# RWKV6 attention into a two-layer block: one more pair of feature tiles by 15 products in the last block, its sums two steps later, its copies on GpSimd

## The chip, the cores and the metric

One core of one Trainium2 chip. The metric is the device time of one execution in microseconds (us), the median of several runs. A profile is one more execution, recorded by the hardware.

## The reference

```
state = wt[:, :, :, None] * state + kt (x) vt          # attention, 768 positions in sequence
y[:, :, t] = rt . (state + (u * kt) (x) vt)
x = y as (3072 tokens, 384)
h = x @ w_in                                            # w_in 384 x 2048
g = h - tanh(h)
out = g @ w_out                                         # w_out 2048 x 384
```

All of it is float32. There are 4 batches, 8 heads, 768 positions and a head size of 48, so x has 3072 rows of 384.

## The kernel before, in words

**Blocks and steps.** The 3072 tokens are cut into eight blocks of 384 tokens (L1112, L1261). A block has 16 steps (L1271), one for each tile of 128 features; step f of a block is written as f 12, f 13 and so on below. In a step TensorE multiplies the block's x with one tile of w_in (`first`, L881 to L888: three matmuls of 128x384, in the PSUM tile hp). ScalarE copies hp to h. From h, ScalarE and VectorE make g (`slight`, L894 to L918). In most steps the squares are ScalarE's (lines 906, 907 and 909). In the last two steps of the last block the square s = h*h is VectorE's, with a maximum beside it (the line 914), and only then ScalarE squares once more (L917). Then come two VectorE products of 128x384 (L891): h = h*s, and g from qa and h. These two are put off by a step: they stand in the list `rest` of the next step.

**The second layer in two forms.** g @ w_out is done plainly (`Second`, L954 to L995): for each of three tiles of 128 tokens a matmul of 128x384 a feature tile, the third split into two of 192. Or it is done for a pair of feature tiles at once (`Fewer`, L997 to L1063): the 3x2 blocks of g and the 2x3 blocks of w_out are added and subtracted beforehand (VectorE, L932 for g, `form_g`), then come 15 products of 128x128 in place of 18 (`product`, L1004). Each of the 15 has a place of its own and is accumulated over all pairs. Products 0 to 11 lie in the PSUM banks acc (`add`, L1013, in two parts of six), 12 to 14 in a bank of att (`others`, L1025). At the end of all pairs ScalarE copies the banks to the tile `sums` (L1023), `others_summed` (L1037) adds the last three, and the 12 VectorE operations of `SUMS` (L113, run at L1046) turn the 15 places into nine blocks of 128x128, which `PLACES` (L119) lists.

**The last block.** Blocks 1 to 6 take `Fewer` for all 16 steps. The last takes it for f 0 to 9, five pairs (`LAST = 5`, L75, L234), and plain for f 10 to 15. So its sums must be joined: once they are ready `gathered` (L1054) copies the nine blocks into rows in the tile G (six copies), and `added` (L982) adds those rows at the last feature tile (L993, VectorE, one input from PSUM, one from G) and sends the rows out (L995).

**What sets the order.** TensorE, VectorE, ScalarE and SyncE run their instructions in the order in which the program writes them (`manual_schedule`, L1114); GpSimd is not in that list, but a data dependence holds for it too. In each step the program writes the step's `first`, then VectorE's list `ops`, then what is `due`. A product of a pair, or a plain feature tile, is due two steps after its g is begun (L1315, L1317). L1299 to L1305 choose how `rest`, the forms and the others are woven in `ops`; `between(a, b)` takes one of each in turn. At L1324 to L1331 the last block gets its `others`, its sums in two halves and its copies. At f 14 come three VectorE operations that test earlier results (L1334, L1250, L1251). After the last step come two more of them (L1384), a matmul of one column that counts (L1386), the last `rest`, and `again` (L1389), which the engines read at L1393 ahead of the second and third tile of tokens. The last two plain feature tiles are written there, tile of tokens by tile of tokens (L1395).

Of the kernel before, what the change touches and what calls it, by code (L numbers as in the profile page):

```python
# [68 lines left out]
NF = FF // P  # L69
# [2 lines left out]
AHEAD = 6  # L72
RAWS = 5
LAG = 2
LAST = 5  # L75
PIECES = 0, 0, 2, 3, 3, 2, 4, 4, 3, 3, 3, 4, 4
UNITS = [(0, 0), (0, 1)] + [u for j in range(NF // 2 - 2) for u in ((1, j), (0, j + 2))] + [(1, NF // 2 - 2),
                                                                                      (1, NF // 2 - 1)]
# [34 lines left out]
SUMS = (("sub", (15, 6, 10), (0, 0, 6)), ("sub", (2, 2, 5), (3, 5, 3)),  # L113
        ("add", (6, 7, 13), (1, 7, 1)), ("add", (7, 9, 14), (5, 9, 11)),
        ("sub", (10, 10, 14), (5, 5, 6)), ("add", (11, 12, 11), (10, 2, 10)),
        ("sub", (14, 4, 14), (11, 3, 11)), ("add", (2, 8, 13), (10, 5, 10)),
        ("add", (13, 4, 13), (2, 2, 15)), ("add", (8, 8, 12), (4, 4, 12)),
        ("add", (0, 4, 0), (11, 2, 11)), ("sub", (14, 14, 1)))
# [8 lines left out]
def kernel(  # L127
# [12 lines left out]
    nc = tc.nc  # L140
# [46 lines left out]
    def draw(names, cols):  # L187
        nc.gpsimd.memset(mask_all[0:L, cols], 1.0)
        for m in names:
# [5 lines left out]
            else:  # L195
# [10 lines left out]
                   in_=start[:, 0:BANK].unsqueeze(1).to_broadcast([P, 2 * NPAIR * NCP * L // BANK, BANK]))  # L206
# [26 lines left out]
    fast = range(1, blocks_n)  # L233
    few = [0 if i not in fast else NF if i + 1 < blocks_n else 2 * LAST for i in range(blocks_n)]  # L234
    n_whole = blocks_n * NPAIR * NCH
# [62 lines left out]
    def scratch(ps):  # L298
        return ps.tile([P, 2, BANK], F32, name="att", tag="att")
# [594 lines left out]
    def slight(h, n, i, f):  # L894

        s, qa = (dense.tile([P, NB], F32, name=name, tag=name) for name in ("s", "qa"))
        q, j = divmod(f, 2)
        if i in fast:  # L900
            g = G[:, g_at(q, "0" + "ab"[j]):g_at(q, "2" + "ab"[j]) + 1].rearrange("p t c -> p (t c)")
        else:
            g = ring(sums, 0, n)
        if n in light:
            at = 2 * blocks_n + light.index(n)
            nc.scalar.activation(out=s, in_=h, func=AF.Square)  # L906
            nc.scalar.activation(out=qa, in_=s, func=AF.Square, bias=shift[:, 4:5])  # L907
            junk = work.tile([P, UP * NCH * LP], BF16, name="junk", tag="junk", bufs=1)
            nc.scalar.activation(out=junk[:, 0:NB], in_=s, func=AF.Relu, bias=shift[:, 5:6],  # L909
                                 accum_out=excess[:, at:at + 1])  # L910
            square = first = []
        else:
            at = plain.index(n)
            square = [lambda: nc.vector.tensor_tensor_reduce(
                out=s, in0=h, in1=h, scale=1.0, scalar=0.0, op0=ALU.mult, op1=ALU.max,
                accum_out=top[:, at:at + 1])]
            first = [lambda: nc.scalar.activation(out=qa, in_=s, func=AF.Square, bias=shift[:, 4:5])]  # L917
        return g, first, square, [product(h, h, TOP, s, ALU.mult), product(g, qa, REST, h, ALU.add)]  # L918
# [78 lines left out]
    class Fewer:  # L997
# [56 lines left out]
        def gathered(self):  # L1054

            for i, k, n, src in self.pieces():
                nc.scalar.copy(out=G[:, 6 + 3 * i + k:6 + 3 * i + k + n], in_=src)
            return [G[:, 6 + 3 * i:9 + 3 * i].rearrange("p t c -> p (t c)") for i in range(NB // P)]

        def store(self):  # L1060
# [67 lines left out]
    def converting(pieces, n):  # L1128

        made = []  # L1130
        for _ in range(n):
            if not pieces:
                on_act, on_dve = convert(*raws.pop(0))
                pieces += zip(on_act, ([], [], on_dve))
            op, then = pieces.pop(0)
            op()
            made += then
        return made
# [95 lines left out]
    ahead_of_h, rest, formed, extra, behind, due, summed = [], [], [], [], [], [], []  # L1234
    held_back, forming, late = [], [], []

    def between(ops, others):

        n = min(len(ops), len(others))
        return [op for pair in zip(ops, others) for op in pair] + ops[n:] + others[n:]  # L1240
# [12 lines left out]
    def form_w(n, q, k):  # L1253

        by = w_out_sb.rearrange("p (q j) (k c) -> p q j k c", j=2, c=P)
        op, *of = W_FORMS[n]
        a, b = (by[:, q:q + k, "ab".index(x[0]), int(x[1])] if isinstance(x, str) else forms[:, q:q + k, x]
                for x in of)
        nc.vector.tensor_tensor(out=forms[:, q:q + k, n], in0=a, in1=b, op=OPS[op])

    for i, blk in enumerate(blocks):  # L1261
# [7 lines left out]
        fewer = Fewer(row0, acc, few[i] // 2) if few[i] else None  # L1269
        second = Second(row0, acc, few[i]) if few[i] < NF else None  # L1270
        for f in range(NF):  # L1271
# [11 lines left out]
            g, ahead_of_h, square, later_ops = slight(h, now, i, f)  # L1283
# [6 lines left out]
                              if of and not name.startswith("bound")]  # L1290
            if i:
                spare += [lambda n=n: form_w(n, 4 if f < 12 else 6, 2) for n in formed_w.get(f, ())]
            if not now:
                ops = square + converting(pieces, 2)
            elif now == 1:
                ops = rest + late + square + converting(pieces, 3)
            elif not i:
                ops = extra + square + (rest + behind + spare if f < 7 else rest[:1] + behind + spare + rest[1:])
            elif forming:  # L1299
                ops = between(rest, forming[:2]) + square + formed + forming[2:]  # L1300
                ops = (between(ops, behind) if len(behind) > 2 else ops + behind) + spare
            elif square:
                ops = (between(rest, behind) if len(behind) > 2 else rest + behind) + square + formed + extra + spare
            else:
                ops = between(rest + formed, behind + spare)  # L1305
            for op in ops:
                op()
            rest, behind, formed, forming, held_back = later_ops, [], [], held_back, []
# [7 lines left out]
            else:  # L1316
                due.append((now + LAG + (not i), second.add if later else second.added, (f, g)))  # L1317
            if fewer and second and f == 2 * LAST:
                sure = scratch(ps_a)
# [3 lines left out]
            if fewer and second:  # L1323
                if f == 2 * LAST + 1:  # L1324
                    fewer.others(ps_a, range(4, LAST))
                    behind.append(fewer.others_summed)
                elif f in (2 * LAST + 2, 2 * LAST + 3):
                    for op in fewer.sum(*((0, 6) if f % 2 == 0 else (6, len(SUMS)))):
                        op()
                elif f == 2 * LAST + 4:  # L1330
                    second.rows = fewer.gathered()  # L1331
            if not later and f == NF - 2:
                at = n_whole + n_excess
# [17 lines left out]
            if i == 0 and f == NF - 3:  # L1351
# [3 lines left out]
                G = wide.tile([P, 32, P], F32, name="g", tag="g")  # L1355
# [31 lines left out]
    for op in ahead_of_h + rest:  # L1387
        op()
    nc.vector.tensor_single_scalar(again, sure[0:1, 0, 0:1], float(P * (n_whole + n_excess + n_top)),  # L1389
                                   op=ALU.not_equal)  # L1390
# [9 lines left out]
    with tc.If(anew > 0, label="anew"):  # L1400
        with tc.manual_schedule(engines={PE, SP, DVE, ACT}), ExitStack() as again_pools:
# [7 lines left out]
            for blk in [Block(b, q) for b in range(B) for q in range(NQ)]:  # L1409
                blk.general(ps_a)  # L1410
                second = Second(blk.b * S + blk.q * NB, acc)
# [56 lines left out]
```

## Time and profile before

| | |
|---|---|
| median of 3 runs | 544.04 us (544.01 to 545.4) |
| the profiled execution | 543.88 us |
| its span in the profile | 542.2 us, so 1.68 us lie around the span |
| TensorE, VectorE, ScalarE, GpSimd busy | 534.0, 459.3, 404.2, 7.0 us |
| granted TensorE clock | 0.999 |

A row of a timeline gives the start, the duration, the engine, the line of the kernel, the operation, what it writes and reads, and the count of instructions put together in the row. In brackets stands the idle time of the engine in front of it and who ended that. An "x6" of TensorE at L883 is three matmuls: each float32 matmul shows two records. PEld is the loading of weights. A line of the chain of waits has start, length, engine, tile, line and records.

### The profile page before, as it was taken

How to read it: one execution, taken by the hardware profiler on the slowest of the kernel's cores; microseconds unless marked ns; L12 is line 12 of the kernel's file. 1: busy time of each engine (PE TensorE's matmuls, PEld its weight loads, DVE VectorE, ACT ScalarE, POOL GpSimd, SP SyncE). 2: the span in 40 equal slices, each digit the busy share in tenths (PEclk: the TensorE clock that was granted, in tenths of full speed). 3: DMA queues.
4: the chain of work that ended last, by engine and by line, in shares of the span. 5: the costliest groups of instructions: out<-in, count | busy, mean ns of one | idle time of the engine just before them, and what ended most of it. 6: DMA issues, size and time to landing. Idle time of an engine off the chain costs nothing.

```text
span 542.2 us, 14874 instructions
## 1 busy us (share of the span) xinstructions
PE 534.0 (98%) x5682; PEld 403.4 (74%) x5682; DVE 459.3 (85%) x943; ACT 404.2 (75%) x814; POOL 7.0 (1%) x51
## 2 busy tenths in 40 slices
PE   8999999999999999999999999999999999999996
PEld 5756665678787777877887787877788788777874
DVE  7999999999989989798997989879797997557563
ACT  4999996897668886688767886688766885766561
POOL 1100000000000000000000000000000000000000
PEclk9999999999999999999999999999999999999999
DMA  7799642342311642154122622135321510100101
GB/s 276 242 403 348 219 119 71 122 112 81 106 48 46 162 118 57 44 148 119 61 56 87 132 92 70 50 102 145 90 84 45 118 31 3 56 1 0 45 1 47
DMA packets 53048, 56.34 MB, mean 104 GB/s; under 512 B 21488, under 2 KB 50928, under 8 KB 52976
## 3 DMA queue, kind: packets, MB, share of 16 engines
q1 hardware_dynamic: 52592, 55.18, 33.5%
q8 instruction: 48, 0.79, 0.6%
q14 instruction: 24, 0.20, 0.1%
q10 hardware_dynamic: 288, 0.10, 0.1%
q0 software_dynamic: 96, 0.07, 0.1%
HBM read 44.73 MB, written 4.72 MB: 91 GB/s over the span
## 4 chain that ended last, share of the span: by engine, by line
PE 95%; DVE 2%; DMA 1%; issue 0%; PEld 0%; SPq 0%; PEldq 0%; DVEq 0%
PE hp L883 44%; PE acc L1011 27%; PE att L1011 7%; PE acc L962 5%; PE att L769 4%; PE att L494 2%; PE acc L989 2%; PE att L575 1%; PE att L883 1%; DMA r<-in_rT 1%; PE acc L883 1%; DVE scores L502 1%; DVE post L429 0%; PE att L989 0%; PEld att L679 0%
## 5 line engine op out<-in xcount | busy, mean ns | idle before, releaser
L883 PE MATMUL hp<-xT,w_sb 128*128 128x384 f32 x738 | 259.2, 487 | 0.5 <-DVE w_sb L268 0.5
L883 PEld LDWEIGHTS hp<-xT,w_sb 128*128 128x128 f32 x738 | 131.9, 190 | 69.7 <-issue 0.6
L1011 PE MATMUL acc<-forms,g 128*128 128x128 f32 x954 | 133.2, 276 | 0.0
L888 ACT ACTIVATE h<-hp 128x384 f32<-128x384 f32 x123 | 60.4, 491 | 97.2 <-PE hp L883 97.1
L1011 PEld LDWEIGHTS acc<-forms,g 128*128 128x128 f32 x954 | 122.0, 192 | 10.3
L891 DVE SCALAR_TENSOR_TENSOR h<-h,s 128x384 f32<-128x384 f32 x128 | 70.6, 552 | 51.6 <-ACT s L906 51.5
L932 DVE TENSOR_TENSOR g<-g 128x256 f32<-128x256 f32 x265 | 103.4, 420 | 7.3 <-PE acc L1011 6.5
L907 ACT ACTIVATE qa<-s,shift 128x384 f32<-128x384 f32 x113 | 69.5, 615 | 3.7
L909 ACT ACTIVATE junk<-s,shift 128x384 bf16<-128x384 f32 x113 | 67.7, 599 | 0.0
L891 DVE SCALAR_TENSOR_TENSOR g<-qa,h 128x384 f32<-128x384 f32 x112 | 61.7, 551 | 1.6 <-ACT qa L917 0.2
L906 ACT ACTIVATE s<-h 128x384 f32<-128x384 f32 x113 | 59.1, 523 | 3.5
L1011 PEld LDWEIGHTS acc<-w_sb,g 128*128 128x128 f32 x318 | 46.7, 191 | 9.7 <-ACT sums L979 0.3
L1011 PE MATMUL acc<-w_sb,g 128*128 128x128 f32 x318 | 53.0, 276 | 0.0
L1011 PE MATMUL att<-w_sb,g 128*128 128x128 f32 x212 | 35.5, 275 | 0.0
L1011 PEld LDWEIGHTS att<-w_sb,g 128*128 128x128 f32 x212 | 31.1, 192 | 5.3
L1046 DVE TENSOR_TENSOR sums<-sums 128x256 f32<-128x256 f32 x84 | 32.9, 407 | 1.7 <-ACT sums L1023 1.4
L962 PE MATMUL acc<-w_sb,sums 128*128 128x384 f32 x96 | 33.7, 487 | 0.0
L264 ACT ACTIVATE up<-raw 128x768 f16<-128x768 f32 (+1 forms) x32 | 33.1, 1074 | 0.0
L962 PEld LDWEIGHTS acc<-w_sb,sums 128*128 128x128 f32 x96 | 18.0, 190 | 12.3 <-DVE sums L891 0.3
L417 DVE TENSOR_TENSOR_SCAN pre<-w,start 128x780 f32<-128x780 f32 x14 | 25.0, 1783 | 0.8
L429 DVE TENSOR_TENSOR_SCAN post<-w,seed 128x780 f32<-128x780 f32 x14 | 24.9, 1776 | 0.0
L909 ACT ACTIVATION_READ_ACCUMULATOR junk<-s,shift 128x1 f32 x113 | 21.1, 186 | 0.0
(119 smaller groups left out, 530.5 us busy)
## 6 DMA issues: line engine op xcount, KB each, us to landing
raw<-in_weights SPq DMA_DIRECT2D x16, 768.0 KB, 7.0
w<-in_wT SPq DMA_DIRECT2D x7, 780.0 KB, 4.5
k<-in_kT SPq DMA_DIRECT2D x7, 768.0 KB, 4.6
r<-in_rT SPq DMA_DIRECT2D x7, 768.0 KB, 4.5
v_sb<-in_v SPq DMA_DIRECT2D x8, 576.0 KB, 3.9
k<-in_tokens SPq DMA_DIRECT2D x7, 576.0 KB, 5.0
r<-in_tokens SPq DMA_DIRECT2D x7, 576.0 KB, 4.8
out_y<-sums SPq DMA_DIRECT2D x18, 128.0 KB, 1.8
```

The lines of the kernel that those rows point to most:

```text
L264: return lambda: nc.scalar.activation(out=to, in_=of, func=AF.Copy, scale=scale, bias=bias)
L417: return nc.vector.tensor_tensor_scan(out=self.tile("pre")[:, cols], data0=self.tile("w")[:, cols], data1=start[:, 0:n * NCH * LP], initia ...
L883: nc.tensor.matmul(hp, lhsT=w_in_sb[:, f, kc, :], rhs=xT[kc], start=(kc == KC - 1), stop=(kc == 0))
L888: return h, nc.scalar.activation(out=h, in_=hp, func=AF.Copy, scale=1.0 / UPSCALE)
L891: return lambda: nc.vector.scalar_tensor_tensor(out=out, in0=in0, scalar=scalar, in1=in1, op0=op0, op1=ALU.mult)
L906: nc.scalar.activation(out=s, in_=h, func=AF.Square)
L907: nc.scalar.activation(out=qa, in_=s, func=AF.Square, bias=shift[:, 4:5])
L909: nc.scalar.activation(out=junk[:, 0:NB], in_=s, func=AF.Relu, bias=shift[:, 5:6], accum_out=excess[:, at:at + 1])
L932: return lambda: nc.vector.tensor_tensor(out=G[:, to:to + 2], in0=two(G, g_at(q, a0), g_at(q, a1)), in1=two(G, g_at(q, b0), g_at(q, b1)), ...
L962: nc.tensor.matmul(acc, lhsT=g[:, j * P:(j + 1) * P], rhs=w_out_sb[:, f, :], start=(f == self.first), stop=(f == NF - 1))
L1011: nc.tensor.matmul(to, lhsT=G[:, g_at(q, a), :], rhs=rhs, start=start, stop=stop, skip_group_check=True)
L1046: ops.append(lambda op=op, at=at: nc.vector.tensor_tensor(out=at[0], in0=at[1], in1=at[2], op=OPS[op]))
```

## The change

`LAST` goes from 5 to 6. So f 10 and f 11 of the last block are no plain feature tiles but a sixth pair by 15 products, and the steps that are named by LAST move: the taking of `sure` from f 10 to f 12, and `others` for the last pairs, with `others_summed` behind it, from f 11 to f 13. The 12 operations of `SUMS` were written behind `ops` of f 12 and f 13, six each. Now they stand inside `ops` of f 14 and f 15: at f 14 four of them ahead of the square and two behind it, at f 15 six operations and the two of `rest`, woven, ahead of the square. `gathered` moves from f 14 to f 15, and its six copies from ScalarE to GpSimd.

```diff
-LAST = 5
+LAST = 6
@@ gathered
             for i, k, n, src in self.pieces():
-                nc.scalar.copy(out=G[:, 6 + 3 * i + k:6 + 3 * i + k + n], in_=src)
+                nc.gpsimd.tensor_copy(out=G[:, 6 + 3 * i + k:6 + 3 * i + k + n], in_=src)
@@ the steps
+            adding = []
+            if fewer and second and f > 2 * LAST + 1:
+                adding = fewer.sum(*((0, 6) if f % 2 == 0 else (6, len(SUMS))))
...
                 ops = (between(ops, behind) if len(behind) > 2 else ops + behind) + spare
+            elif adding and f % 2:
+                ops = adding[:2] + between(adding[2:], rest) + square
+            elif adding:
+                ops = between(rest, behind) + adding[:4] + square + adding[4:]
             elif square:
...
                 if f == 2 * LAST + 1:
                     fewer.others(ps_a, range(4, LAST))
                     behind.append(fewer.others_summed)
-                elif f in (2 * LAST + 2, 2 * LAST + 3):
-                    for op in fewer.sum(*((0, 6) if f % 2 == 0 else (6, len(SUMS)))):
-                        op()
-                elif f == 2 * LAST + 4:
+                elif f == NF - 1:
                     second.rows = fewer.gathered()
```

## The prediction

> **What bounds the kernel now.** I read the page first, for the busy shares and the chain that ended last.
>
> ```profile
> PE 534.0 (98%) x5682; PEld 403.4 (74%) x5682; DVE 459.3 (85%) x943; ACT 404.2 (75%) x814; POOL 7.0 (1%) x51
> PE 95%; DVE 2%; DMA 1%; issue 0%; PEld 0%; SPq 0%; PEldq 0%; DVEq 0%
> ```
>
> TensorE (PE) is busy for 98% of the span and holds 95% of the chain. That speaks for any cut in its work. But 98% is a mean over eight blocks, and the change touches only the end of the last, so I read next the chain in order of time from f 10's products on.
>
> ```profile
> 511.01 1.34 PE acc L1011 x12
> 512.35 1.94 PE hp L883 x6
> 514.29 0.67 PE att L1011 x6
> 514.95 2.68 PE acc L1011 x24
> 517.63 1.94 PE hp L883 x6
> 519.57 1.61 PE acc L989 x6
> 521.19 0.33 PE att L989 x2
> 521.51 1.94 PE hp L883 x6
> ...
> 531.20 1.61 PE acc L989 x6
> 532.81 0.33 PE att L989 x2
> 533.14 0.12 PE att L1386 x2
> 533.26 3.17 PE acc L989 x10
> ...
> 537.11 0.68 DVE g L993 x2
> ```
>
> The rows join end to end: up to 533 us the last block is TensorE's. f 11's first layer starts at 512.35, f 12's at 517.63; a plain step is 1.94 first layer, 1.61 + 0.33 second. Behind 533.14 I no longer trust the chain alone: there the last g is still being made. So the third view is VectorE's (DVE) timeline.
>
> ```profile
> 518.34 2.47 DVE L1046 TENSOR_TENSOR sums<-sums 128x256 f32<-128x256 f32 x6 [1.45 <-ACT sums L1023]
> ...
> 527.88 0.56 DVE L914 CUSTOM_DVE_ANT_0 s<-h 128x384 f32<-128x384 f32 x1 [2.10 <-ACT h L888]
> ...
> 528.37 0.23 DVE L1334 TENSOR_SCALAR holds<-excess 128x129 bf16<-128x129 f32 x1
> ...
> 529.12 0.55 DVE L891 SCALAR_TENSOR_TENSOR h<-h,s 128x384 f32<-128x384 f32 x1
> 529.90 0.56 DVE L891 SCALAR_TENSOR_TENSOR g<-qa,h 128x384 f32<-128x384 f32 x1 [0.23 <-ACT qa L917]
> 531.76 0.56 DVE L914 CUSTOM_DVE_ANT_0 s<-h 128x384 f32<-128x384 f32 x1 [1.30 <-ACT h L888]
> ...
> 532.56 0.16 DVE L1251 TENSOR_REDUCE count<-ends 128x1 f32<-128x3 f32 x1
> 532.63 0.55 DVE L891 SCALAR_TENSOR_TENSOR h<-h,s 128x384 f32<-128x384 f32 x1
> 533.28 0.56 DVE L891 SCALAR_TENSOR_TENSOR g<-qa,h 128x384 f32<-128x384 f32 x1
> ...
> 534.85 0.56 DVE L993 SCALAR_TENSOR_TENSOR g<-acc,g 128x384 f32<-128x384 f32 x1 [0.95 <-PE acc L989]
> ...
> 533.89 0.30 PEld L989 LDWEIGHTS acc<-w_sb,g 128*128 128x128 f32 x2 [0.41 <-DVE again L1389]
> ```
>
> Call the start of the last square X: 531.76. From X on VectorE's work is a fixed string: count ends at X + 0.96, g at X + 2.08 (533.28 + 0.56 = 533.84), and TensorE loads that g for f 15's first tile of tokens at X + 2.13, after 0.41 us without a load. (The row names `again`; g, which the load reads, was done just ahead.) The first joining operation (L993) starts at X + 3.09, the last pair at X + 5.35. So in the end part **two limits nearly tie**: TensorE comes out of f 13's products at 533.14 and has 0.12 and one 0.65 us product before it wants g, which is there at 533.84. Whichever is late sets the end. In front of X VectorE stood idle for 1.30 us, for h. That slack is what the change spends.
>
> **The change part by part.**
>
> *TensorE.* Out go two plain feature tiles, 2 x (1.61 + 0.33) = 3.88 us. In come 15 products of 128x128, 30 records; the row of 12 is 1.34, 24 are 2.68, so 30 are 3.34. Gain 0.54. In order: f 11 ends its first layer at 514.29, then six products of pair 4 (1.34) and f 12's first layer (1.94) to 517.57, six more products and f 13's to 520.84, then the `others` of two pairs (1.34) and pair 5's products (2.67) to 524.85. So f 14's first layer ends at 526.79 (before: 527.32), f 15's at 530.67 (531.20), f 13's plain products at 532.61 (533.14). Each 0.54 earlier, if nothing else waits.
>
> *VectorE, forms.* Five more operations on g for pair 5, at f 11 to f 13. They are done ahead of their products: the square-free steps leave VectorE idle (1.45 us in front of 518.34), and pair 5's products begin 1.34 us behind the first layer, after `others`. Cost 0; without that cover a part of 5 x 0.42.
>
> *The sums.* They need pair 5's banks, which ScalarE copies behind the products. For their rhythm I need single operations, and for h the row of ScalarE:
>
> ```profile
> 518.34 0.43 DVE L1046 TENSOR_TENSOR sums<-sums 128x256 f32<-128x256 f32 x1 [1.45 <-ACT sums L1023]
> 518.68 0.42 DVE L1046 TENSOR_TENSOR sums<-sums 128x256 f32<-128x256 f32 x1
> ...
> 521.42 0.56 DVE L891 SCALAR_TENSOR_TENSOR g<-qa,h 128x384 f32<-128x384 f32 x1
> 521.89 0.42 DVE L1046 TENSOR_TENSOR sums<-sums 128x256 f32<-128x256 f32 x1
> ...
> 522.23 0.42 DVE L1046 TENSOR_TENSOR sums<-sums 128x256 f32<-128x256 f32 x1
> 522.68 0.42 DVE L1046 TENSOR_TENSOR sums<-sums 128x256 f32<-128x256 f32 x1
> ...
> 527.36 0.49 ACT L888 ACTIVATE h<-hp 128x384 f32<-128x384 f32 x1 [1.58 <-PE hp L883]
> 516.52 1.78 ACT L1023 ACTIVATE sums<-acc 128x512 f32<-128x512 f32 x3
> ```
>
> An operation of the sums holds VectorE for 0.34 us, or 0.45 where it reads what the one in front wrote (522.23 to 522.68); a product of 384 holds it for 0.47 (521.42 to 521.89). Before, the sums began 0.71 behind the last product (517.63 to 518.34; ScalarE's copies end at 518.30). So the first starts at 524.85 + 0.71 = 525.56, the fourth at 526.69, VectorE is free at 527.03. f 14's h is there at 526.79 + 0.56 = 527.35 (before: 527.32 to 527.88), so f 14's square is not held up. It takes 0.49 (527.88 to 528.37). Then the fifth and sixth sum, 0.45 + 0.34, to 528.63; then the three tests, 0.75 (528.37 to 529.12), to 529.38. At f 15 stand six sums and two products ahead of the square: 0.34, 0.45, 0.34, the product 0.47, 0.34, the product 0.47, 0.34, 0.34 = 3.09. f 14's qa is ready well before (its ScalarE no longer copies rows). **So the last square starts at 532.47 instead of 531.76.** Its h is ready at 530.67 + 0.56 = 531.23: VectorE's queue, not h, is what it waits for now, by 1.24 us. In sum eight sums (2.94) went in front of the last square, behind the one before it; 1.30 and 0.23 of idle time and the 0.54 that f 14's square comes earlier pay for a part only.
>
> *Behind X.* Count, g, and the rest keep their distances, since they are VectorE's string: TensorE, out of f 13's products at 532.61, waits for the count until about X + 1, does f 14's first tile (0.65), and gets g at X + 2.13. Queued behind its waiting count are all the last products; every store hangs on them. So the end moves with X: **+0.71 us**. TensorE's 0.54 is lost as waiting.
>
> *GpSimd's copies.* ScalarE loses six copies that lay beside TensorE's work: gain 0. GpSimd (POOL) gets six.
>
> ```profile
> L171 POOL MEMSET start<- 128x780 f32 x1 | 0.8, 754 | 0.0
> L200 POOL COPY mask_all<-mask_all 64x128 int8<-64x128 int8 x1 | 0.3, 286 | 0.1
> masks.py:197 POOL MEMSET ident<- 128x128 f32 x1 | 0.2, 205 | 0.3 <-POOLq L1460 0.3
> L1057 ACT COPY g<-sums x6: 298/348/407, 527.7 to 528.9; 128x256 f32<-128x256 f32 x3, 128x128 f32<-128x128 f32 x3
> ```
>
> No float32 copy of GpSimd is in this trace. The nearest row is its COPY, 0.29 us for 128 columns; 128 columns more cost (754 - 205) / 652 x 128 = 0.11 by the two memsets, so 0.29 and 0.40 is my estimate, 2.1 us for six. They can begin when the ninth row-building sum (index 9) has ended, at 531.4, and the last when the twelfth has, at 532.5. The first joining operation wants two of them at 532.47 + 3.09 = 535.56, the last all six at 537.82. I take cost 0: at 0.3 to 0.4 us they are through by 534.6. Below nothing is excluded, for nothing on the path ends earlier by a copy that was hidden. The upper bounds are the rivals' below.
>
> Sum: 542.2 + 0.71 + 1.68 around the span = 544.6 for a profiled run of 543.88; the median is 0.16 above that run, so **544.8 us**.
>
> **The rivals.**
>
> *A: GpSimd's copies and VectorE hold each other up.* The copies run beside the tenth product and the last sums, the last square, and f 15's two products, all of which read two operands from SBUF. If such an operation must let a copy finish, the second g is late by each copy that gets in front. One ahead of a sum costs 0.40, the second ahead of the square 0.29, and the others fit partly into the count's short operations: about +0.7 in all, 545.5. All five that can start ahead of the last g cost 0.40 + 0.29 + 0.40 + 0.29 + 0.29 = 1.67: 546.5. The trace of before shows no GpSimd operation that reads SBUF beside a VectorE product, so it bears out neither side. The Trainium skill, SBUF — State Buffer, section "Who interferes with whom", speaks for this rival: a VectorE operation with two SBUF inputs and a GpSimd operation that reads SBUF exclude each other, and the one that issues second waits for the whole of the first. By that rule the time would be this rival's and not the forecast's, unless it is always GpSimd that comes second; no row of before tests it.
>
> *B: the copies are late.* If one takes t, six from 531.4 end at 531.4 + 6t, and the last joining operation at 537.82 waits from t = 1.07 us on, nearly four times the nearest row. At 1.5 us it waits 2.6 us: 547.4, clearly slower.
>
> *C: TensorE still sets the end, and the change is faster.* If VectorE runs the sums closer together than I counted, or X's slack is larger, the last square waits for h alone: X = 531.23, and the end comes 0.54 earlier, 543.5. It decides if the string between f 14's square and the last is 1.24 us shorter than my 5.1, that is without any waiting of one sum for another and without most of the tests. Against it: each of its durations is a row.
>
> That the change does not do what it says (fewer products) I exclude: 15 for 18 is in the code, at 0.111 us a record in this trace.
>
> **How the numbers follow.** Forecast 0.52, at 544.8 (544.4 to 545.1 by the roundings of eleven spacings). A 0.27, 545.1 to 546.5. B 0.11, C 0.10. The range goes from 544.1 to 546.5: it leaves out C and most of B. About 0.3%, 1.6 us, is what a measurement of this kernel can tell from no change. The forecast is inside; A crosses 545.7 in less than half of its range (0.10), B nearly always (0.09). So slower by over 0.3% 0.20, within 0.78, faster by over 0.3% 0.02 (C gives only 0.1%).
>
> **What would show it.** After the change: f 14's first layer ends 0.5 us earlier than 527.32; VectorE's last square follows a sum without idle time at about 532.5, not "<-ACT h"; TensorE has a gap of about 0.8 to 1 us in front of L1386, ended by VectorE's count, and a second in front of f 15's first product. GpSimd's copies of about 0.3 to 0.4 us lie between 531.4 and 535. If VectorE's sums or products near them last longer than 0.42 and 0.56, or start with gaps, A is at work; if L993 waits for GpSimd, B; if the last square waits for h, C. An added wait ahead of 524.85, of pair 5's products for their forms, would make all of it wrong.

## The result, and the profile after

The changed kernel takes 545.76 us (median of 22 runs, 544.68 to 546.91), the kernel before 544.34 (22 runs, 543.52 to 545.67). The ratio is 1.0026 with a 95% interval of 1.0019 to 1.0034: some 1.4 us slower, about the bound that was named for what can be told from no change.

The runs of either kernel spread over 2 us, more than the effect. The profiles show where much of it can come from. First the chain in order of time of before, then of after, one first layer of the first block in each:

```profile
52.04 2.17 PE hp L883 x6
```

```profile
52.55 2.17 PE hp L883 x6
```

The 0.51 us between them stand ahead of this row, where weights are still being converted and which the change does not touch; from this row to f 11's first layer in the last block it is 460.29 to 460.32 us in all ten profiles of this document. So a time of the last block is read from a mark inside the run: **Y is the start of f 11's first layer in the last block**, 512.35 before and 512.87 after, and X is the start of the last square, as in the prediction. The chain of the changed kernel from Y on:

```profile
512.87 1.94 PE hp L883 x6
514.81 1.34 PE acc L1011 x12
516.15 1.94 PE hp L883 x6
518.08 1.34 PE acc L1011 x12
519.42 1.94 PE hp L883 x6
521.36 1.34 PE att L1011 x12
522.70 2.68 PE acc L1011 x24
525.38 1.95 PE hp L883 x6
```

f 14's first layer starts at Y + 12.51; before it did at Y + 13.04:

```profile
525.39 1.94 PE hp L883 x6
```

TensorE's gain of 0.53 is there, as worked out. Pair 5's products begin at 522.70, Y + 9.83, where the prediction's sum has them, so the five more operations on g hold nothing up. Then VectorE's timeline from the sums on (start, duration, ..., in brackets the idle time in front and who ended it):

```profile
526.08 1.55 DVE L1046 TENSOR_TENSOR sums<-sums 128x256 f32<-128x256 f32 x4 [2.12 <-ACT sums L1023]
527.87 0.56 DVE L914 CUSTOM_DVE_ANT_0 s<-h 128x384 f32<-128x384 f32 x1 [0.24 <-ACT h L888]
...
528.36 0.88 DVE L1046 TENSOR_TENSOR sums<-sums 128x256 f32<-128x256 f32 x2
529.15 0.22 DVE L1338 TENSOR_SCALAR holds<-excess 128x129 bf16<-128x129 f32 x1
...
529.91 1.21 DVE L1046 TENSOR_TENSOR sums<-sums 128x256 f32<-128x256 f32 x3
531.03 0.55 DVE L891 SCALAR_TENSOR_TENSOR h<-h,s 128x384 f32<-128x384 f32 x1
531.50 0.62 DVE L1046 TENSOR_TENSOR sums<-sums 128x256 f32<-128x256 f32 x1
532.04 0.64 DVE L891 SCALAR_TENSOR_TENSOR g<-qa,h 128x384 f32<-128x384 f32 x1
532.60 0.81 DVE L1046 TENSOR_TENSOR sums<-sums 128x256 f32<-128x256 f32 x2
533.34 0.64 DVE L914 CUSTOM_DVE_ANT_0 s<-h 128x384 f32<-128x384 f32 x1
...
534.29 0.58 DVE L891 SCALAR_TENSOR_TENSOR h<-h,s 128x384 f32<-128x384 f32 x1
534.98 0.56 DVE L891 SCALAR_TENSOR_TENSOR g<-qa,h 128x384 f32<-128x384 f32 x1
...
539.15 0.35 DVE L993 SCALAR_TENSOR_TENSOR g<-att,g 128x192 f32<-128x192 f32 x1
```

The last square has no bracket: it follows a sum with no idle time, and no longer waits for h. X is Y + 20.47, against Y + 19.41 before. The last joining operation starts at Y + 26.28, against Y + 25.09 before:

```profile
537.44 0.36 DVE L993 SCALAR_TENSOR_TENSOR g<-att,g 128x192 f32<-128x192 f32 x1
```

So the last block's end is 1.19 us later by VectorE's rows. By the ends of the spans it is about 1.0 (543.7 - 512.87 against 542.2 - 512.35), for behind the last L993 the span lasts some 4.5 us here and 4.8 before; why is open. The 1.4 of the medians agrees with both within the spread of the runs. GpSimd and TensorE beside it, each from its rows in the timeline:

```profile
531.24 1.70 POOL L1057 COPY g<-sums 128x256 f32<-128x256 f32 x3 [70.87 <-DVE sums L1046]
533.27 1.20 POOL L1057 COPY g<-sums 128x128 f32<-128x128 f32 x3 [0.34 <-DVE sums L1046]
```

```profile
534.43 0.09 PEld L1390 LDWEIGHTS att<-ones,count 128*1 128x1 f32 x2 [1.60 <-DVE count L1251]
...
535.60 0.30 PEld L989 LDWEIGHTS acc<-w_sb,g 128*128 128x128 f32 x2 [0.75 <-DVE again L1393]
```

From the moment the copies begin (531.24) the rows of VectorE are longer and further apart: a sum of 0.62, products of 0.64. Up to 531.03 they are those of before. And TensorE's weight loads stand idle 1.60 us in front of the count's (0.23 before) and 0.75 for g (0.41 before): what it had gained is waited away.

### The profile page after: what moved, and what is told of

Same layout as the page of the kernel before. It is cut to its first block, busy times and chain, and to the rows that moved or that the text cites. A ratio compares the mean times of both kernels' runs of the same rounds, so it can differ in the third digit from the quotient of the medians.

```text
span 543.7 us, 14916 instructions
## 1 busy us (share of the span) xinstructions
PE 533.8 (98%) x5696; PEld 404.1 (74%) x5696; DVE 461.0 (85%) x948; ACT 402.5 (74%) x808; POOL 9.8 (2%) x57
## 4 chain that ended last, share of the span: by engine, by line
PE 90%; DVE 3%; DMA 2%; ACT 2%; issue 1%; POOL 0%; PEldq 0%; PEld 0%; DVEq 0%; POOLq 0%
PE hp L883 43%; PE acc L1011 27%; PE att L1011 7%; PE acc L962 4%; PE att L769 4%; PE att L494 2%; DMA raw<-in_weights 2%; PE att L575 1%; ACT up L264 1%; PE att L305 1%; DVE pre L417 1%; PE acc L989 1%; DVE sums L1046 0%; ACT w_sb L264 0%; PE att L312 0%
## 5 line engine op out<-in xcount | busy, mean ns | idle before, releaser
L1011 PE MATMUL acc<-forms,g 128*128 128x128 f32 x972 | 135.7, 276 | 0.0
L1011 PEld LDWEIGHTS acc<-forms,g 128*128 128x128 f32 x972 | 124.3, 192 | 10.6
L932 DVE TENSOR_TENSOR g<-g 128x256 f32<-128x256 f32 x270 | 105.2, 419 | 7.4 <-PE acc L1011 6.5
L1011 PE MATMUL acc<-w_sb,g 128*128 128x128 f32 x324 | 54.1, 276 | 0.0
```

What stands on the lines that cost most here:

```text
L932: return lambda: nc.vector.tensor_tensor(out=G[:, to:to + 2], in0=two(G, g_at(q, a0), g_at(q, a1)), in1=two(G, g_at(q, b0), g_at(q, b1)), ...
L1011: nc.tensor.matmul(to, lhsT=G[:, g_at(q, a), :], rhs=rhs, start=start, stop=stop, skip_group_check=True)
```

## The experiments

The theories: P, VectorE's longer string in front of the last square costs about 0.6, and GpSimd's reads beside it lengthen that string by another half microsecond. Q, the string alone; the stretched rows are no part of it. The others are named in the expectations. Each kernel ran 12 times, beside runs of the kernel before; its ratio to before is good to 0.10 to 0.15%, or 0.5 to 0.8 us, so the verdicts rest on X - Y and on the last L993, each from one profile a kernel; in the four kernels where they should agree they do to 0.00 and 0.03. What the span lasts behind the last L993, some 4.5 to 4.8 us in the ten profiles, is in no column but the ratio's.

| kernel | Y | X - Y | last L993 - Y | ratio to before, 95% interval |
|---|---|---|---|---|
| before | 512.35 | 19.41 | 25.09 | |
| changed | 512.87 | 20.47 | 26.28 | 1.0026 (1.0019 to 1.0034) |
| no copies | 514.01 | 19.97 | 25.64 | 1.0007 (0.9992 to 1.0022) |
| memsets | 513.25 | 19.97 | 25.67 | 1.0008 (0.9995 to 1.0020) |
| ScalarE copies | 513.08 | 19.97 | 25.66 | 1.0001 (0.9990 to 1.0013) |
| early tests | 514.22 | 19.84 | 25.66 | 1.0010 (0.9998 to 1.0022) |
| before, GpSimd copies | 513.22 | 19.41 | 25.12 | 1.0007 (0.9995 to 1.0019) |
| held GpSimd copies | 513.28 | 19.97 | 25.67 | 1.0015 (1.0005 to 1.0025) |
| both mends | 513.81 | 19.34 | 25.04 | 0.9999 (0.9988 to 1.0010) |
| both, late sums | 512.75 | 18.88 | 24.58 | 0.9992 (0.9980 to 1.0005) |

**Without the copies.**

```diff
-            for i, k, n, src in self.pieces():
-                nc.gpsimd.tensor_copy(out=G[:, 6 + 3 * i + k:6 + 3 * i + k + n], in_=src)
```

> The changed kernel with GpSimd's six copies left out (the rows added at the end are then whatever lies in those places). Y is the start of f 11's first layer in the last block, X the start of the last square; X - Y was 19.41 us before and is 20.47 after. Theory P (VectorE's longer string costs about 0.6 and GpSimd's reads beside it another 0.45 to 0.65): X - Y about 20.0, every sum 0.42 and every product 0.56, the end about 0.6 earlier than in the changed kernel, +0.7 to +0.8 against before. Rival Q (the string alone, the copies cost nothing): X - Y stays 20.4 to 20.5 and the time that of the changed kernel, +1.4.

The chain's row of Y, and rows of VectorE's timeline:

```profile
514.01 1.94 PE hp L883 x6
```

```profile
532.17 0.55 DVE L891 SCALAR_TENSOR_TENSOR h<-h,s 128x384 f32<-128x384 f32 x1
532.64 0.42 DVE L1046 TENSOR_TENSOR sums<-sums 128x256 f32<-128x256 f32 x1
532.97 0.55 DVE L891 SCALAR_TENSOR_TENSOR g<-qa,h 128x384 f32<-128x384 f32 x1
533.44 0.62 DVE L1046 TENSOR_TENSOR sums<-sums 128x256 f32<-128x256 f32 x2
533.98 0.55 DVE L914 CUSTOM_DVE_ANT_0 s<-h 128x384 f32<-128x384 f32 x1
...
539.65 0.36 DVE L993 SCALAR_TENSOR_TENSOR g<-att,g 128x192 f32<-128x192 f32 x1
```

From f 14's first product to X it is 1.81 us here and 2.31 with the copies (531.03 to 533.34): 0.50 of the loss belongs to the copies, and the last L993 starts 0.64 earlier. Against before 0.56 of X's delay stay, with no GpSimd at work: VectorE's string. P holds, Q falls.

**Writes without reads.** The copies become memsets, each made to wait for the sum that its copy waited for.

```diff
-                nc.gpsimd.tensor_copy(out=G[:, 6 + 3 * i + k:6 + 3 * i + k + n], in_=src)
+                begin_behind(self.made[n_sum], nc.gpsimd.memset(G[:, 6 + 3 * i + k:6 + 3 * i + k + n], 0.0))
```

> The six copies replaced by six GpSimd memsets of the same places and sizes, each made to wait for the sum that its copy waited for: GpSimd writes and does not read (the rows are lost). Theory P with reads as the cause: as without copies, X - Y about 20.0, the stretched products back to 0.56. Rival W (GpSimd beside VectorE costs by its writes or its semaphores): X - Y 20.3 to 20.5, rows of VectorE stretched as in the changed kernel. Rival Q: 20.4 to 20.5 with no row stretched.

GpSimd's rows of the timeline and VectorE's last square:

```profile
531.60 0.47 POOL L1061 MEMSET g<- 128x256 f32 x2 [70.86 <-PE hp L883]
532.36 0.32 POOL L1061 MEMSET g<- 128x256 f32 x1 [0.28 <-DVE sums L1047]
533.16 0.60 POOL L1061 MEMSET g<- 128x128 f32 x3 [0.49 <-DVE sums L1047]
```

```profile
533.22 0.55 DVE L914 CUSTOM_DVE_ANT_0 s<-h 128x384 f32<-128x384 f32 x1
```

GpSimd is busy for 1.39 us between 531.60 and 533.76, beside the same sums and products (the copies were for 2.90), and X - Y is 19.97 to the hundredth (Y is 513.25). Writes and semaphores cost nothing here: W falls, it is the reads. The rule of the Trainium skill, SBUF — State Buffer, "Who interferes with whom", says so too: two SBUF inputs of VectorE contend with a GpSimd instruction that reads SBUF, not with one that only writes it. The trace agrees (0.50 with reads, 0.00 with writes). By the prediction's reading of that page of the Trainium skill the later one waits for the whole of the first. That is not decided here. No operation of VectorE lost more than 0.21 (the sum of 0.62, with 0.54 to the next start in place of 0.33), less than the 0.30 to 0.40 of a copy that nothing disturbs (below); but an operation that comes while a copy is under way would wait only for what is left of it.

**The copies on ScalarE, behind the last qa.**

```diff
-                nc.gpsimd.tensor_copy(out=G[:, 6 + 3 * i + k:6 + 3 * i + k + n], in_=src)
+                nc.scalar.copy(out=G[:, 6 + 3 * i + k:6 + 3 * i + k + n], in_=src)
...
     for op in ahead_of_h + rest:
         op()
+    second.rows = fewer.gathered()
```

> The same copies on ScalarE, written behind the last step's qa, so that they stand in front of nothing. Theory P: X - Y about 20.0, the end +0.7 to +0.8 against before, no L993 waiting for a copy (1.6 us of copies start about X + 1.3, the first two done by X + 2.1, wanted at X + 3.1). Rival Q: +1.2 to +1.4 as in the changed kernel. If the copies come late, L993 waits for ScalarE and the time is above +1.4.

```profile
533.05 0.55 DVE L914 CUSTOM_DVE_ANT_0 s<-h 128x384 f32<-128x384 f32 x1
...
538.74 0.35 DVE L993 SCALAR_TENSOR_TENSOR g<-att,g 128x192 f32<-128x192 f32 x1
```

With Y at 513.08 that is 19.97 and 25.66: the whole computation at the times of the kernel without copies. No L993 waits for ScalarE. The run times alone would not show it: the ratio gives 0.05 us above before (0.5 below to 0.7 above), where 0.7 to 0.8 above was expected.

**The three tests earlier.**

```diff
-                ops = between(rest, behind) + adding[:4] + square + adding[4:]
+                ops = between(rest, behind) + [tested] + adding[:4] + square + adding[4:]
```

(`tested` holds the three operations of f 14, which go from their old place.)

> The changed kernel with the three tests of f 14 (0.75 us) moved ahead of the first sums, where VectorE stood idle for 2.12 us. If VectorE's string sets the end (P and Q alike), X - Y falls by 0.75 to about 19.7 and the end by as much: +0.5 to +0.7 against before. Rival T (TensorE or the last copies set the end, the string only looks late): X moves, the time stays at +1.2 to +1.4.

```profile
529.70 2.13 DVE L1046 TENSOR_TENSOR sums<-sums 128x256 f32<-128x256 f32 x5
531.75 0.55 DVE L891 SCALAR_TENSOR_TENSOR h<-h,s 128x384 f32<-128x384 f32 x1
...
534.06 0.64 DVE L914 CUSTOM_DVE_ANT_0 s<-h 128x384 f32<-128x384 f32 x1
...
539.88 0.35 DVE L993 SCALAR_TENSOR_TENSOR g<-att,g 128x192 f32<-128x192 f32 x1
```

Y is 514.22. X falls by 0.63 and the last L993 by 0.62: the string sets the end, T falls. The expected 0.75 was too much by 0.12, and the row says why: with the tests gone the sixth sum and the seventh, which reads it, are neighbours and must wait for each other (five sums in 2.05, from 529.70 to 531.75, where the changed kernel needed 0.79 for two, from 528.36 to 529.15, and 1.12 for three, from 529.91 to 531.03). From the first product to X it is still 2.31: the stretch by GpSimd is unchanged.

**The copies alone, in the kernel before.**

```diff
-                nc.scalar.copy(out=G[:, 6 + 3 * i + k:6 + 3 * i + k + n], in_=src)
+                nc.gpsimd.tensor_copy(out=G[:, 6 + 3 * i + k:6 + 3 * i + k + n], in_=src)
```

> The kernel before with nothing but its six copies moved from ScalarE to GpSimd (five pairs, sums where they were). There the copies fall behind the twelfth sum, near f 12's two products, with over a microsecond of idle time of VectorE behind them. Theory P: one or two VectorE operations that read two operands last 0.64 instead of 0.56 or start late, X - Y stays 19.41 and the time that of before. Rival Q: no row is stretched, time as before. Rival W2 (copies on GpSimd cost time wherever they are): +0.3 or more.

```profile
524.10 2.96 POOL L1057 COPY g<-sums 128x256 f32<-128x256 f32 x6 [63.38 <-DVE sums L1046]
```

```profile
526.10 0.69 DVE L891 SCALAR_TENSOR_TENSOR g<-qa,h 128x384 f32<-128x384 f32 x1
528.76 0.56 DVE L914 CUSTOM_DVE_ANT_0 s<-h 128x384 f32<-128x384 f32 x1 [1.96 <-ACT h L888]
...
532.63 0.56 DVE L914 CUSTOM_DVE_ANT_0 s<-h 128x384 f32<-128x384 f32 x1 [1.40 <-ACT h L888]
```

The product beside the copies lasts 0.69 instead of 0.56, but 1.96 us of idle time follow it. X - Y is 19.41, as before (Y is 513.22). The same collision costs nothing where VectorE has slack.

**The copies on GpSimd, held back** until VectorE's last product.

```diff
     for op in ahead_of_h + rest:
-        op()
+        made_last = op()
+    second.rows = fewer.gathered(made_last)
...
-                nc.gpsimd.tensor_copy(out=G[:, 6 + 3 * i + k:6 + 3 * i + k + n], in_=src)
+                begin_behind(then, nc.gpsimd.tensor_copy(out=G[:, 6 + 3 * i + k:6 + 3 * i + k + n], in_=src))
```

> The changed kernel with the six GpSimd copies held back until the last product of VectorE has ended: the same reads of SBUF, but beside no VectorE operation with two SBUF operands. Theory P: X - Y 19.97 as without copies, the last L993 at Y + 25.65, no stretched row, copies of 0.25 to 0.4 each, done before their L993; against the changed kernel -0.6. If GpSimd's reads cost VectorE also at L993 (one operand from PSUM): L993 longer than 0.56. If the copies are late: L993 waits for GpSimd and the last starts after Y + 26.

The group's row of this line (its durations are min, median and max in ns), and VectorE's rows:

```profile
L1057 POOL COPY g<-sums x6: 296/346/403, 535.4 to 536.8; 128x256 f32<-128x256 f32 x3, 128x128 f32<-128x128 f32 x3
```

```profile
533.25 0.55 DVE L914 CUSTOM_DVE_ANT_0 s<-h 128x384 f32<-128x384 f32 x1
...
536.41 0.56 DVE L993 SCALAR_TENSOR_TENSOR g<-acc,g 128x384 f32<-128x384 f32 x1 [1.02 <-POOL g L1057]
```

Alone, a copy takes 0.30 for 128 columns and 0.40 for 256, as was estimated. X - Y is 19.97, the joining operation keeps its 0.56 beside a copy (one of its operands is in PSUM), and the last starts at Y + 25.67. The first L993 is named as waiting for GpSimd, but it starts at X + 3.16, where it stands with ScalarE's copies too (X + 3.15). The ratio, 1.0015, is the highest of the kernels with a Y + 25.66; their intervals overlap, and its interval overlaps that of the changed kernel too.

**Both mends**: the tests early, the copies on ScalarE (the diffs of the third and fourth experiment together).

> Two mends together: the three tests ahead of the first sums, and the copies on ScalarE behind the last qa. If string and port add up as the single runs say (20.47 - 0.50 - 0.63), X - Y is 19.34 and the last L993 starts at Y + 25.0, against Y + 25.09 before: the time of before within 0.1. If the two hide each other, X - Y stays near 19.7.

```profile
533.15 0.55 DVE L914 CUSTOM_DVE_ANT_0 s<-h 128x384 f32<-128x384 f32 x1
...
538.85 0.35 DVE L993 SCALAR_TENSOR_TENSOR g<-att,g 128x192 f32<-128x192 f32 x1
```

With Y at 513.81: 19.34 and 25.04, what the single runs add up to. VectorE's string and GpSimd's reads (the port of the expectation) are separate terms.

**And the last two sums behind the last test**, into VectorE's pause in front of the first L993.

```diff
-                ops = adding[:2] + between(adding[2:], rest) + square
+                ops, last_sums = adding[:2] + between(adding[2:-2], rest) + square, adding[-2:]
...
                                    op=ALU.not_equal)
+    run(last_sums)
+    second.rows = fewer.gathered()
```

(The copies stand behind these sums and in another order: the three that need neither of them come first.)

> As the one with both mends, and the last two sums behind the last product and the count's test, where VectorE waits for the first L993 anyway. Then f 15's h ends the last wait: X - Y 18.9, the last L993 at Y + 24.55 if TensorE's 0.54 comes through: 0.5 faster than before. If the copies, now behind those sums, are late, the first or the last L993 waits for ScalarE and the gain is smaller or gone (Y + 25.1 or later).

```profile
531.63 0.56 DVE L914 CUSTOM_DVE_ANT_0 s<-h 128x384 f32<-128x384 f32 x1
...
533.70 0.60 DVE L1046 TENSOR_TENSOR sums<-sums 128x256 f32<-128x256 f32 x2
534.79 0.56 DVE L993 SCALAR_TENSOR_TENSOR g<-acc,g 128x384 f32<-128x384 f32 x1 [0.48 <-PE acc L989]
...
537.33 0.35 DVE L993 SCALAR_TENSOR_TENSOR g<-att,g 128x192 f32<-128x192 f32 x1
```

```profile
532.93 0.09 PEld L1390 LDWEIGHTS att<-ones,count 128*1 128x1 f32 x2 [0.23 <-issue]
```

Y is 512.75, so X is Y + 18.88 and the last L993 Y + 24.58, 0.51 before the kernel before. The last square starts 0.04 behind the end of ScalarE's copy of h (531.59), and TensorE no longer waits for the count: its 0.23 us of idle time are those of the kernel before. TensorE's gain comes through once VectorE does not stand in its way. The ratio, 0.9992 (0.9980 to 1.0005), does not tell it from the kernel before, but its interval lies below that of the changed kernel.

## Why the prediction was right or wrong

*Two limits nearly tie* was right. The end hangs on X in every kernel: the last L993 starts between X + 5.67 and X + 5.82 in all ten. What sets X differs. It is h, and so TensorE's f 15, in the kernel before, in the same with GpSimd's copies, and in the one with late sums; in the other seven it is VectorE's queue.

*TensorE's 0.54* was right in size (0.53 at f 14) and right in being lost: the waits named in front of L1386 (now L1390) and of f 15's first product are there. The first was to be 0.8 to 1 us; it is 1.60, and 1.01 in the kernel without copies.

*X moves by 0.71* was nearly right: without the copies' reads it moves by 0.56. The term that was too large is the string between f 14's square and the last: 4.97 in the kernel without copies (529.01 to 533.98) against 5.12 worked out. Nearly all of it, 0.14, is the twelfth sum, 128 columns wide, which I gave the 0.34 of 256 columns: it starts at 533.78 there, and the square 0.20 behind it.

*GpSimd's copies at cost 0* is the step that failed. Their length was right for copies that nothing disturbs (0.30 and 0.40), and so was that no joining operation waits for them. But the cost is not in their own time. Reading SBUF beside VectorE's sums, products and square, they delay X by 0.50 and the last L993 by 0.64 in all. That is rival A, to which I gave 0.27 and about 0.7 us: the trace of before had no row for it, the Trainium skill had the rule (SBUF — State Buffer, "Who interferes with whom"), and I left the sum without it. That A's 0.7 is met so closely is in part luck: it was two whole copies in front of two operations (0.40 + 0.29), and the rows show smaller delays of more operations, 0.21 at the sum of 0.62, 0.09 at the product behind it, 0.20 at the last two sums, and the rest behind X. They also began 0.7 us sooner than I said: at 531.24 - 0.52 = 530.72 against 531.4, behind an earlier sum than the one of their first place in the program; GpSimd's order is not among those written out by hand.

Rival B did not happen. Rival C, TensorE setting the end, needed the string 1.24 shorter; the last experiment made it 3.88 (527.75 to 531.63) in place of 5.12, and the 0.5 came.

So forecast plus A is what happened: 0.56 + 0.50 at X, 1.19 at the last L993. The measured 545.76 lies in the range, but only because the range took in rival A: it is above the forecast's own 544.4 to 545.1. It is 1.0 above the forecast, 0.3 of it because the kernel before stands at 544.34 over 22 runs and at 544.04 over the three that were shown.

## What to carry to other kernels

A cut in the busiest engine's work comes through only as far as the next engine has slack where the cut falls: read, at the end of the program, how long each operation in front of the last dependence stood idle, and count what is moved into that place. Copies put on an idle engine are not free because the engine is; ask what they read while a critical engine reads two operands. Here the same copies cost 0.6 us beside a full queue of VectorE. Ahead of its idle time, behind its last product and on ScalarE they cost nothing that X or the last L993 shows.

## What was not expected of the hardware

- GpSimd and VectorE stretch each other: beside two-operand operations a 128x256 copy took up to 0.72 us and a 128x384 product 0.58 to 0.69, alone 0.40 and 0.55.
- A sum that reads what the one in front wrote starts 0.45 behind it (522.23 to 522.68 before), one that has nothing to do with it 0.34 (518.34 to 518.68): moving three tests out from between two of them gained 0.63, not 0.75.
- What stands ahead of that first layer near 52 us puts profiles up to 1.9 us apart: Y lies between 512.35 and 514.22 in the ten, while X - Y agrees to 0.01 in the four kernels where it should.
